# Linear attention into a multiplicative FFN: all loads on one queue, the weight fold first, full-height attention matmuls

## The chip, the cores and the metric

The kernel runs on one core of one Trainium2 chip. The metric is device time in microseconds: 260.99 us is the median of three executions of the kernel before (260.66 to 261.18). A profile of one execution has a span of 258.1 us, counted from its first to its last instruction; the measured time is 2.9 us longer than that span.

## The reference

Inputs are f32: q, k, v of shape (8 batches, 8 heads, 576 tokens, 64), w1 and w2 of shape (512, 1024), w3 of shape (1024, 1024), w_out of shape (1024, 512). The output is (4608, 512) in f32.

```python
def phi(x):
    return np.where(x > 0, x, np.exp(x) - 1.0) + 1.0
q_p, k_p = phi(q), phi(k)
kv  = np.einsum('bhsd,bhse->bhde', k_p, v)
z   = np.sum(k_p, axis=2)
num = np.einsum('bhsd,bhde->bhse', q_p, kv)
den = np.einsum('bhsd,bhd->bhs', q_p, z)[..., None] + 1e-06
attn = num / den                              # (8, 8, 576, 64)
x = attn.transpose(0, 2, 1, 3).reshape(4608, 512)
a, b = x @ w1, x @ w2
out = ((a * b) @ w3) @ w_out
```

Two things are used by both kernels. The last two products have nothing between them, so w3 @ w_out is multiplied once into a 1024x512 matrix `wf` (the fold), for which w3 must be transposed. And phi(x) = max(x + 1, min(exp(x), 1)) = min(max(x, 0) + 1, exp(x)).

## The kernel before

Each batch has 576 tokens: 512 are held as four tiles of 128 ("J", j = 0 to 3), the other 64 are the rest ("R"), and two rests make one more tile of 128. The 36 tiles go through the FFN in 9 chunks of 4. A list of steps, `ORDER`, fixes the order of the instructions on every engine; each engine executes its own in that order. The parts that the change touches:

```python
ld = ctx.enter_context(tc.tile_pool(name="ld", bufs=5))    # raw q, k, v of a batch, 1 MB each; w3 too
mm_ps = ... bufs=4   # PSUM, one bank each
at_ps = ... bufs=2   # PSUM, two banks each

def load_qkv(name, src, b, part, alt=False):     # q, k, v on SyncE's queue
    ...
    return nc.sync.dma_start(out=..., in_=src[b, h0:h1, 0:NJ * P, :]...)
def load_w12(x): ...  nc.gpsimd.dma_start(...)   # weights: GpSimd's queue, f32 to bf16 on the way
def load_wo(x):  ...  nc.gpsimd.dma_start(...)
def load_w3(i):  ...  nc.gpsimd.dma_start(...)

# phi: exp on ScalarE, then two steps on VectorE
nc.scalar.activation(out=e, in_=x, func=AF.Exp)                      # L137, 1024 elements, e in bf16
nc.vector.tensor_scalar_min(out=e, in0=e, scalar1=1.0)               # L141, bf16
nc.vector.scalar_tensor_tensor(                                      # L162, 256 elements, x in f32
    out=out, in0=x, scalar=1.0, in1=e, op0=ALU.add, op1=ALU.max)

def kv_half(b, g):     # batches 1 to 7: 64-row matmuls in pairs, two partial sums
    for n, (kk, vv, halves) in enumerate(steps):
        for r in halves:
            rows = slice(r * R, (r + 1) * R)
            nc.tensor.matmul(kvp[:, r, i * W:(i + 1) * W], kk[rows], vv[rows], ...)     # L199
    nc.scalar.copy(out=kvf, in_=kvp[:, 0, 0:2 * W])                                     # L203
    nc.vector.tensor_tensor(out=kvs[b]..., in0=kvf, in1=kvp[:, 1, 0:2 * W], op=ALU.add) # L204

def nat_units(b, js):  # numerator and denominator of a tile: 8 matmuls of 64 rows x 65 columns
    for hp in range(KC):
        for u in range(2):
            nc.tensor.matmul(nd[0:n, u, ...], w[rows], kvs[b][rows, hp, u, :], ...)     # L265
    # VectorE: add 1e-6 (L271), reciprocal (L273), multiply (L275), grouped for two tiles

def xt_tr(b, j): ...   # x transposed on TensorE (L285): batches 1 and 3
def xt_load(b, part): ... nc.sync.dma_start(out=dst, in_=src, transpose=True)   # batches 2, 4 to 7, rests
def q_tr(b, g): ...    # q transposed on TensorE (L309): batches 0 to 3; by DMA (qt_load) in 4 to 7
def first_nd(hp, own): # batch 0 alone: masked kv against q, the result is x already transposed
    ...                # L330; 1/den as exp(-ln(den)) on ScalarE

def f_unit(c, f):      # 4 matmuls for a, 4 for b (L371); a copied (L376); a * b on VectorE (L377)
def o_unit(c, m):      # 8 matmuls with wf (L390), copy to SBUF (L393), store on SyncE (L400)
def o_last(c, m):      # the last tile in two halves, stored on two queues (L417, L420)
def w3_tr(i): ...      # 8 transposes of w3 on TensorE (L454), copy (L455)
def wf_mm(i, part): .. # 8 matmuls, w3t against w_out (L464), copy (L467)
```

At the start, ORDER interleaves the load and the work of batch 0 with the fold: w3 rows 0 to 3 and w_out are asked for at the beginning, w3 rows 4 to 7, w1 and w2 later, beside q, k and v.

Of the kernel before, what the change touches and what calls it, by code (L numbers as in the profile page):

```python
# [13 lines left out]
P = 128  # L14
# [4 lines left out]
def kernel(  # L19
# [14 lines left out]
    NTOK = B * S  # L34
# [5 lines left out]
    JW = H * NJ * D  # L40
    RW = (H // 2) * D
    n_chunks = NTOK // NCH

# [3 lines left out]
    for b in range(0, B, 2):  # L47
        for key in [("J", b, j) for j in range(NJ)] + [("J", b + 1, j) for j in range(NJ)] + [("R", b, 0)]:
            tile_of[key] = len(order)
            order.append(key)  # L50
        tile_of["R", b + 1, 0] = tile_of["R", b, 0]
# [5 lines left out]
    ldr = ctx.enter_context(tc.tile_pool(name="ldr", bufs=8))  # L57
    setup = ctx.enter_context(tc.tile_pool(name="setup", bufs=2))
    phi_p = ctx.enter_context(tc.tile_pool(name="phi", bufs=1))
    e_p = ctx.enter_context(tc.tile_pool(name="e", bufs=2))  # L60
    att = ctx.enter_context(tc.tile_pool(name="att", bufs=2))
    lr = ctx.enter_context(tc.tile_pool(name="lr", bufs=2))
    ab_p = ctx.enter_context(tc.tile_pool(name="ab", bufs=2))
    sm = ctx.enter_context(tc.tile_pool(name="sm", bufs=3))
# [3 lines left out]

    ident = consts.tile([P, P], BF16)
    mask = consts.tile([P, 2, 2, D], BF16)  # L70
    eps = consts.tile([P, 1], F32)
    zero = consts.tile([P, NCH], BF16)

    w1_sb = wpool.tile([P, KC, DFF], BF16)
    w2_sb = wpool.tile([P, KC, DFF], BF16)
    wo_sb = wpool.tile([P, FC, DM], BF16)
    wf_sb = wpool.tile([P, FC, DM], BF16)
    xt = wpool.tile([P, NT, KC, P], BF16)
    vt = wpool.tile([P, NJ, H, D + 1], BF16)
    vr = wpool.tile([P, H // 2, D + 1], BF16)  # L80

    def constants(part):
        if part == 0:
            make_identity(nc, ident)
        elif part == 1:

            nc.gpsimd.memset(mask, 0.0)
            nc.gpsimd.memset(mask[0:D, :, 0, :], 1.0)
            nc.gpsimd.memset(mask[D:P, :, 1, :], 1.0)
            nc.gpsimd.memset(eps, 1e-6)  # L90
            nc.gpsimd.memset(vt[:, :, :, D:D + 1], 1.0)
            nc.gpsimd.memset(vr[:, :, D:D + 1], 1.0)
        else:
            nc.vector.memset(zero, 0.0)

    def warm_up(n):

        ps = mm_ps.tile([P, NCH], F32, tag="mm", name="warm")
        for _ in range(n):
            nc.tensor.matmul(ps, zero[:, 0:P], zero, start=True, stop=True)  # L100


    raw = {}

    def load_qkv(name, src, b, part, alt=False):


        if part == 3:
            t = raw[name + "r", b] = ldr.tile([P, RW], F32, tag="ldr", name=f"{name}32r")
            for hh in range(2):  # L110
                (nc.gpsimd if alt else nc.sync).dma_start(  # L111
                    out=t[hh * R:(hh + 1) * R].rearrange("p (h d) -> p h d", d=D),
                    in_=src[b, hh * 4:(hh + 1) * 4, NJ * P:S, :].rearrange("h p d -> p h d"))
            return None
        if (name, b) not in raw:
            raw[name, b] = ld.tile([P, JW], F32, tag="ld", name=f"{name}32")
        t = raw[name, b]
        h0, h1 = ((0, 4), (4, 8), (0, 8))[part]
        W = NJ * D
        return nc.sync.dma_start(  # L120
            out=t[:, h0 * W:h1 * W].rearrange("p (h x) -> p h x", x=W),
            in_=src[b, h0:h1, 0:NJ * P, :].rearrange("h (p j) d -> p h (j d)", j=NJ))


    ph = {}

    es = {}

    def phi_exp(name, b, g):

        if g == 2:
            x, e = raw[name + "r", b], e_p.tile([P, RW], BF16, tag="er", name="er")
        else:
            x = raw[name, b][:, g * (JW // 2):(g + 1) * (JW // 2)]
            e = e_p.tile([P, JW // 2], BF16, tag="e", name="e", bufs=4)
        es[name, b, g] = x, e
        nc.scalar.activation(out=e, in_=x, func=AF.Exp)  # L137

    def phi_min(name, b, g):
        e = es[name, b, g][1]  # L140
        nc.vector.tensor_scalar_min(out=e, in0=e, scalar1=1.0)  # L141

    def phi_max(name, b, hp):

        if (name, b) not in ph:
            ph[name, b] = [None, None]
        if hp == KC:
            dr = ph[name, b][1] = phi_p.tile([P, RW], BF16, tag=name + "r", name=name + "r", bufs=3)
            todo = [(dr, *es[name, b, 2])]
        else:  # L150
            if hp == 0:
                ph[name, b][0] = phi_p.tile([P, KC, NJ, 2, D], BF16, tag=name + "j", name=name + "j")
            dj = ph[name, b][0]
            x, e = es[name, b, hp // 2]
            W = NJ * D
            todo = []
            for u in range(2):
                h = 2 * (hp % 2) + u
                todo.append((dj[:, hp, :, u, :], *(t[:, h * W:(h + 1) * W].rearrange(
                    "p (j d) -> p j d", d=D) for t in (x, e))))  # L160
        for out, x, e in todo:
            nc.vector.scalar_tensor_tensor(  # L162
                out=out, in0=x, scalar=1.0, in1=e, op0=ALU.add, op1=ALU.max)

    def copy_of(alt):
        return nc.vector.tensor_copy if alt else nc.scalar.copy

    def v_unit(b, i, alt=False):

        if i < 2:  # L170
            copy_of(alt)(  # L171
                out=vt[:, :, 4 * i:4 * i + 4, 0:D],
                in_=raw["v", b].rearrange("p (h j d) -> p j h d", h=H, j=NJ)[
                    :, :, 4 * i:4 * i + 4])
        else:
            copy_of(alt)(out=vr[:, :, 0:D], in_=raw["vr", b].rearrange("p (h d) -> p h d", d=D))


    kvs, qts, xns = {}, {}, {}

    def kv_half(b, g):


        kj, kr = ph["k", b]
        if g == 0:
            kvs[b] = att.tile([P, KC, 2, D + 1], BF16, tag="kv", name="kv")
        kvp = at_ps.tile([P, 2, 512], F32, tag="at", name="kvp")
        W = 2 * (D + 1)
        for i in range(2):
            hp = 2 * g + i  # L190
            steps = [(kj[:, hp, j].rearrange("p u d -> p (u d)"),
                      vt[:, j, 2 * hp:2 * hp + 2, :].rearrange("p h e -> p (h e)"), (0, 1))
                     for j in range(NJ)]
            steps.append((kr[:, i * P:(i + 1) * P],
                          vr[:, 2 * i:2 * i + 2, :].rearrange("p h e -> p (h e)"), (g,)))
            for n, (kk, vv, halves) in enumerate(steps):
                for r in halves:
                    rows = slice(r * R, (r + 1) * R)
                    nc.tensor.matmul(  # L199
                        kvp[:, r, i * W:(i + 1) * W], kk[rows], vv[rows],  # L200
                        start=(n == 0), stop=(n == (NJ if r == g else NJ - 1)))
        kvf = lr.tile([P, 2 * W], F32, tag="kvf", name="kvf")
        nc.scalar.copy(out=kvf, in_=kvp[:, 0, 0:2 * W])  # L203
        nc.vector.tensor_tensor(  # L204
            out=kvs[b][:, 2 * g:2 * g + 2].rearrange("p a u e -> p (a u e)"), in0=kvf,
            in1=kvp[:, 1, 0:2 * W], op=ALU.add)

    def kv_full(b, g):

        kj, kr = ph["k", b]  # L210
        if g == 0:
            kvs[b] = att.tile([P, KC, 2, D + 1], BF16, tag="kv", name="kv")
        kvp = at_ps.tile([P, 2, 512], F32, tag="at", name="kvp")
        W = 2 * (D + 1)
        rows = slice(g * R, (g + 1) * R)
        for i in range(2):
            hp = 2 * g + i
            for j in range(NJ):
                nc.tensor.matmul(kvp[:, 0, i * W:(i + 1) * W],
                                 kj[:, hp, j].rearrange("p u d -> p (u d)"),  # L220
                                 vt[:, j, 2 * hp:2 * hp + 2, :].rearrange("p h e -> p (h e)"),
                                 start=(j == 0), stop=False)
            nc.tensor.matmul(kvp[:, 0, i * W:(i + 1) * W], kr[rows, i * P:(i + 1) * P],
                             vr[rows, 2 * i:2 * i + 2, :].rearrange("p h e -> p (h e)"),
                             start=False, stop=True)
        return kvp[:, 0, 0:2 * W]

    def kv_copy(b, g, p, alt=False):
        copy_of(alt)(out=kvs[b][:, 2 * g:2 * g + 2].rearrange("p a u e -> p (a u e)"), in_=p)


    def qt_load(b, part):
        qj, qr = ph["q", b]
        if part == 0:
            t = att.tile([P, KC, NJ * P], BF16, tag="qt", name="qt")
            src = qj.rearrange("p c j u d -> p (c j u d)")
            dst = t.rearrange("p c (j t) -> p (c j) t", t=P)
        else:
            t = att.tile([P, 2, P], BF16, tag="qtr", name="qtr", bufs=3)
            src, dst = qr, t  # L240
        qts[b, part] = t
        nc.sync.dma_start(out=dst, in_=src, transpose=True)

    def nat_units(b, js):


# [384 lines left out]
```

## Time and profile before

| | busy us | share of the span |
|---|---|---|
| TensorE matmul (PE) | 237.4 | 92% |
| TensorE weight load (PEld) | 116.2 | 45% |
| VectorE (DVE) | 167.9 | 65% |
| ScalarE (ACT) | 129.0 | 50% |
| GpSimd (POOL) | 21.1 | 8% |

HBM read is 38.80 MB, written 9.44 MB. The queue table counts 48.98 MB, as the bytes land: weights are read as f32 and land as bf16, at half their size, and transposes by DMA inside the chip are counted too. The page cuts the span into 40 slices of 6.45 us, with a digit for the busy tenths of each engine in each; matmuls are pipelined, so the spacing of their starts says more than the length of one. TensorE's granted clock is full in all slices.

### The profile page before, as it was taken

What the parts mean: (1) busy time and instruction counts of PE and PEld (TensorE: products, weight loads), DVE (VectorE), ACT (ScalarE), POOL (GpSimd) and SP (SyncE); (2) the same over time, 40 slices, a digit from 0 to 9 for tenths busy, and PEclk for the clock granted to TensorE, in tenths of its full rate; (3) what the DMA queues carried; (4) which work ended last, traced back from release to release, by engine and by line L of the source; (5) the groups of instructions that cost most, each with busy time, mean ns of one, the idle gap of its engine ahead of it and who ended that gap; (6) DMA issues with size and microseconds to landing.
All of it is one profiled execution on the core that took longest, in us unless ns stands there. A gap on an engine that the chain in (4) does not pass through costs nothing.

```text
span 258.1 us, 4507 instructions
## 1 busy us (share of the span) xinstructions
PE 237.4 (92%) x1656; PEld 116.2 (45%) x1673; DVE 167.9 (65%) x426; ACT 129.0 (50%) x205; POOL 21.1 (8%) x42
## 2 busy tenths in 40 slices
PE   1138999999999999999999999999999999999994
PEld 1124554545454454455444444444444444444442
DVE  0025787969978979997968589468866543423320
ACT  2048587858478664677353645726533203331421
POOL 8000765000101000000000000000000000000000
PEclk9999999999999999999999999999999999999999
DMA  6999999999898599939988975934980124003024
GB/s 100 200 257 378 316 229 245 208 334 307 302 291 250 87 340 215 307 104 253 211 193 245 369 160 123 248 99 131 218 220 26 34 57 124 0 37 125 3 82 163
DMA packets 70085, 48.98 MB, mean 190 GB/s; under 512 B 34416, under 2 KB 64368, under 8 KB 70064
## 3 DMA queue, kind: packets, MB, share of 16 engines
q1 hardware_dynamic: 63104, 42.54, 61.4%
q0 software_dynamic: 6816, 6.03, 14.1%
q8 instruction: 13, 0.21, 0.3%
q10 hardware_dynamic: 144, 0.13, 0.1%
q14 instruction: 8, 0.07, 0.1%
HBM read 38.80 MB, written 9.44 MB: 187 GB/s over the span
## 4 chain that ended last, share of the span: by engine, by line
PE 84%; DMA 8%; ACT 2%; SPq 1%; issue 1%; DVE 1%; DVEq 0%; POOLq 0%
PE a_ps L371 25%; PE b_ps L371 24%; PE o_ps L390 23%; DMA k<-in_k_dram 4%; DMA w3b<-in_moe_w_dram 4%; PE kvp L199 3%; PE wf_ps L464 3%; PE nd L265 3%; SPq L111 1%; PE tp L309 1%; PE w3p L454 1%; PE xtp L285 1%; PE o_ps L417 1%; DVE qj L162 1%; ACT e L137 0%
## 5 line engine op out<-in xcount | busy, mean ns | idle before, releaser
L371 PEld LDWEIGHTS <-w_sb 128*128 128x128 bf16 x576 | 54.2, 98 | 63.4 <-issue 0.5
L377 DVE TENSOR_TENSOR ab<-a_sb,b_ps 128x512 bf16<-128x512 f32 x72 | 49.0, 684 | 46.6 <-PE b_ps L371 35.4
L371 PE MATMUL a_ps<-xt,w_sb 128*128 128x512 bf16 x288 | 75.1, 380 | 0.1
L371 PE MATMUL b_ps<-xt,w_sb 128*128 128x512 bf16 x288 | 74.9, 379 | 0.0
L376 ACT COPY a_sb<-a_ps 128x512 f32<-128x512 f32 x72 | 41.9, 586 | 56.8 <-PE a_ps L371 55.6
L390 PE MATMUL o_ps<-wf_sb,ab 128*128 128x512 bf16 x266 | 63.2, 379 | 0.7
L390 PEld LDWEIGHTS <-ab 128*128 128x128 bf16 x280 | 26.7, 98 | 30.8
L393 ACT COPY o_sb<-o_ps 128x512 f32<-128x512 f32 x24 | 14.0, 583 | 30.7 <-PE o_ps L390 30.7
L162 DVE SCALAR_TENSOR_TENSOR kj<-k,e 128x256 bf16<-128x256 f32 x64 | 23.6, 417 | 0.1
L162 DVE SCALAR_TENSOR_TENSOR qj<-q,e 128x256 bf16<-128x256 f32 x64 | 23.4, 417 | 0.1
L141 DVE TENSOR_SCALAR e<-e 128x1024 bf16<-128x1024 bf16 x32 | 13.4, 420 | 14.2 <-ACT e L137 14.2
L137 ACT ACTIVATE e<-q 128x1024 bf16<-128x1024 f32 x16 | 16.7, 1058 | 9.3 <-DMA q<-in_q_dram 9.1
L454 PE MATMUL w3p<-ident,w3b 128*128 128x128 bf16 x64 | 6.1, 253 | 15.0 <-ACT w3t L455 8.0
L137 ACT ACTIVATE e<-k 128x1024 bf16<-128x1024 f32 x16 | 16.9, 1056 | 4.1 <-DMA k<-in_k_dram 2.7
L275 DVE TENSOR_TENSOR xn<-nd,r 128x512 bf16<-128x512 f32 x28 | 18.0, 686 | 0.0
L464 PE MATMUL wf_ps<-wo_sb,w3t 128*128 128x512 bf16 x61 | 16.7, 412 | 1.0 <-ACT w3t L455 0.8
L454 PEld LDWEIGHTS <-w3b 128*128 128x128 bf16 x64 | 4.9, 113 | 16.6 <-DMA w3b<-in_moe_w_dram 8.2
L393 DVE COPY o_sb<-o_ps 128x512 f32<-128x512 f32 x11 | 7.6, 688 | 6.4 <-PE o_ps L390 6.4
L171 ACT CAST vt<-v 128x1024 bf16<-128x1024 f32 x9 | 9.3, 1046 | 2.0 <-DMA v<-in_v_dram 2.0
L203 ACT COPY kvf<-kvp 128x260 f32<-128x260 f32 x14 | 5.3, 375 | 8.9 <-PE kvp L199 8.7
L464 PEld LDWEIGHTS <-w3t 128*128 128x128 bf16 x64 | 6.2, 104 | 7.8 <-issue 1.7
L199 PE MATMUL kvp<-vt,kj 64*128 64x130 bf16 x224 | 9.2, 217 | 0.0
(81 smaller groups left out, 163.5 us busy)
## 6 DMA issues: line engine op xcount, KB each, us to landing
out_dram<-o_sb SPq DMA_DIRECT2D x31, 256.0 KB, 3.2
k<-in_k_dram SPq DMA_DIRECT2D x7, 1024.0 KB, 8.6
q<-in_q_dram SPq DMA_DIRECT2D x7, 1024.0 KB, 8.2
v<-in_v_dram SPq DMA_DIRECT2D x6, 1024.0 KB, 7.4
w3b<-in_moe_w_dram POOLq DMA_DIRECT2D x8, 256.0 KB, 7.1
v<-in_v_dram SPq DMA_DIRECT2D x4, 512.0 KB, 8.5
w_sb<-in_moe_w_dram POOLq DMA_DIRECT2D x8, 256.0 KB, 11.3
out_dram<-o_sb SPq DMA_DIRECT2D x9, 128.0 KB, 2.4
```

The costliest lines, as they stand in the source:

```text
L137: nc.scalar.activation(out=e, in_=x, func=AF.Exp)
L141: nc.vector.tensor_scalar_min(out=e, in0=e, scalar1=1.0)
L162: nc.vector.scalar_tensor_tensor(out=out, in0=x, scalar=1.0, in1=e, op0=ALU.add, op1=ALU.max)
L199: nc.tensor.matmul(kvp[:, r, i * W:(i + 1) * W], kk[rows], vv[rows], start=(n == 0), stop=(n == (NJ if r == g else NJ - 1)))
L275: nc.vector.tensor_tensor(out=dst.rearrange("p (c u) e -> p u c e", u=2), in0=v4[:, :, :, 0:D], in1=r[0:n].unsqueeze(3).to_broadcast([n, 2 ...
L371: nc.tensor.matmul(ps, w[:, kc, f * P:(f + 1) * P], xt[:, 4 * c:4 * c + 4, kc, :], start=(kc == 0), stop=(kc == KC - 1))
L376: nc.scalar.copy(out=a_sb, in_=a_ps)
L377: nc.vector.tensor_mul(out=abs_[c][:, f, :], in0=a_sb, in1=b_ps)
L390: nc.tensor.matmul(o_ps, ab[:, f, m * P:(m + 1) * P], wf_sb[:, f, :], start=(f == 0), stop=(f == FC - 1))
L393: copy_of(alt)(out=o_sb, in_=o_ps)
L454: nc.tensor.transpose(tp[:, kc, :], raw["w3", i][:, kc * P:(kc + 1) * P], ident)
L464: nc.tensor.matmul(wfs[i], w3ts[i][:, kc, :], wo_sb[:, kc, :], start=(kc == 0), stop=(kc == FC - 1))
```

## The change

The kernel is written anew around the same arithmetic, with a new ORDER. Its parts:

1. All loads, of q, k, v as well as of weights, are issued from GpSimd's queue, in one order. SyncE's queue keeps transposes and stores.
2. The fold is first: w3 rows 0 to 3, then w_out in four slices; after each slice, four rows of `wf` are taken a step further (`wa`). The other four rows follow when their w3 has landed. Short matmuls on zeros (`warm`) fill the first waits.
3. Attention matmuls use all 128 rows: kv in one accumulation per pair of heads with the rest padded by zeros (`vrz`), and numerator and denominator of a pair of heads together against a block-diagonal `kvb` (130 columns).
4. TensorE transposes q and x for batches 0 to 3, also x of batches 0 and 2; DMA transposes serve batches 4 to 7 and the rests. Batch 0 is computed as the others are.
5. phi is computed as min(max(x, 0) + 1, exp(x)): one step from f32 to bf16, one on two bf16 tensors.

The purpose is to have TensorE start the fold as soon as its data lands, to keep waiting stores and transposes out of the way of loads, and to save a copy and an addition per kv.

```diff
-def load_qkv(...):   nc.sync.dma_start(...)            # 1 MB, 512 KB and 64 KB pieces
+def ld_(n, b, h0, nh, queue):   queue_of[queue].dma_start(...)    # always "g", nc.gpsimd
+def lr(n, b, queue):            # the rest of a batch in one piece of 128 KB
-nc.vector.tensor_scalar_min(out=e, in0=e, scalar1=1.0)
-nc.vector.scalar_tensor_tensor(out=out, in0=x, scalar=1.0, in1=e, op0=ALU.add, op1=ALU.max)
+nc.vector.tensor_scalar(out=d, in0=raw, scalar1=0.0, scalar2=1.0, op0=ALU.max, op1=ALU.add)   # t, 1024
+nc.vector.tensor_tensor(out=d[:, hp], in0=ts, in1=es, op=ALU.min)                             # m, 512, bf16
-kv_half: 36 matmuls of 64 rows a batch, ACT copy and DVE add for each half
+def kv(b, hp):  5 matmuls of 128 rows x 130 columns (4 tiles and the padded rest), 4 of these a batch
+def kc(b, g0, ng, r, eng):  two copies a batch into the diagonal blocks of kvb
-nat_units: 8 matmuls of 64 rows x 65 columns a tile; VectorE's steps grouped for two tiles
+def na(b, hp):  4 matmuls of 128 rows x 130 columns, 4 of these a batch (nar: 4 for the rest)
+def nd(b, hp):  add 1e-6, reciprocal, multiply, one unit at a time
-first_kvz, first_nd, first_rest (batch 0)
+def xp(b, hp), xc(b, hp, eng):  x transposed on TensorE for batches 0 to 3
+def wa(c0, n):  rows 0 to 3 of wf against slices c0 .. c0 + n of w_out
-L0.3 E0 I0 M0.0 x0.2 N0.3 E1 X0.0 w0 y0.2 M1.3 E2 w1 L0.0 ...
+l3:0 const:0 const:6 l3:1 warm:26,0 ... l3:3 lo:0,2 lo:2,2 w3t:0 warm:8,1 lo:4,2 w3c:0,a lo:6,2 ...
+ld:k,0,0,4,g ... lr:k,0,g ... lr:v,0,g wa:0,1 ld:k,0,4,4,g wa:1,1 ... ld:q,0 (2) ... ld:v,0 (3) ...
+l3:6 ... l3:7 ... lw:0,0 lw:1,0 lw:0,1 lw:1,1 ... lw:1,3 ... ld:k,1 lr:k,1 ... lr:v,1 ... ld:q,1 ... ld:v,1 (2)
+... kv:0 ... na:0 nd:0 xp:0 xc:0 ... fk:0,0 f:0,3 f:0,5 f:0,4 f:0,6 f:0,2 f:0,7 f:0,1 qt:1,0 kv:1,0 ...
-... Q8.2
+... ol:8,2 oc:7,1,a st:7,1,s o:8,1 oc:8,1,v st:8,1,s      # the last tile in one piece
```

(`l3` loads a row block of w3, `lo` a slice of w_out, `lw` a quarter of w1 or w2, `ld` and `lr` q, k, v; `f` is a unit of w1 and w2, `o` of wf, `oc` its copy, `st` its store. Most of ORDER and all definitions not spoken of are left out.)

## The prediction

> **What bounds the kernel now.** I read the page's 40 slices first, then the chain of waits in order of time, then the cadence of TensorE in the timeline.
>
> ```profile
> PE   1138999999999999999999999999999999999994
> DVE  0025787969978979997968589468866543423320
> DMA  6999999999898599939988975934980124003024
> GB/s 100 200 257 378 316 229 245 208 334 307 302 291 250 87 340 215 307 104 253 211 193 245 369 160 123 248 99 131 218 220 26 34 57 124 0 37 125 3 82 163
> ```
>
> PE is at 9 from the fifth slice to the last but one. The only slices in which it is not are the first four, up to 25.8 us, in which the DMA engines are full. The chain says the same in time (start, length, what):
>
> ```profile
> 1.24 3.78 DMA w3b<-in_moe_w_dram
> ...
> 9.04 11.36 DMA k<-in_k_dram
> ...
> 25.29 6.50 DMA w3b<-in_moe_w_dram
> ...
> 245.99 6.64 PE o_ps L390 x30
> 252.63 1.76 PE o_ps L417 x16
> ```
>
> So a load ends last until 31.8 us, and after that nearly only TensorE. Is a busy PE at its own rate? The timeline (start, length, what) answers:
>
> ```profile
> 118.27 1.03 PE L371 MATMUL b_ps<-xt,w_sb 128*128 128x512 bf16 x4
> 119.23 0.40 PE L199 MATMUL kvp<-vt,kj 64*128 64x130 bf16 x8
> ...
> 120.35 1.90 PE L390 MATMUL o_ps<-wf_sb,ab 128*128 128x512 bf16 x7
> 122.19 0.42 PE L265 MATMUL nd<-kv,qt 64*128 64x65 bf16 x16
> 122.54 1.04 PE L371 MATMUL a_ps<-xt,w_sb 128*128 128x512 bf16 x4
> 123.41 1.03 PE L371 MATMUL b_ps<-xt,w_sb 128*128 128x512 bf16 x4
> 124.28 1.03 PE L371 MATMUL a_ps<-xt,w_sb 128*128 128x512 bf16 x4
> ```
>
> From 122.54 to 124.28 there are 8 matmuls of 512 columns: 0.216 us each, 0.42 ns a column. Between full-height groups, a batch's kv takes 119.13 (the start 118.27 plus 4 x 0.216) to 120.35, 1.22 us; two tiles of nd take 0.46 us (one of the 8 o_ps records before them is missing from the trace).
>
> All work of PE, in these units: 576 matmuls of w1 and w2, 124.3; 288 of wf, 62.2; 64 of the fold, 13.8; 160 transposes at 0.056 (four take 108.90 to 109.13), 8.9; batch 0 by its own way, 3.1; kv and nd of seven batches, 7 x (1.22 + 2 x 0.46 + 0.34 for the rest) = 17.4; sum 229.7. The last matmul ends at 254.4, so 24.7 us are idle or slow, nearly all before 32 us. That is all the change can win at PE, unless it reduces PE's work.
>
> **What the Trainium skill says.** (1) "TensorEngine Tiling (Array Packing)", section Key Properties: changing the tiling mode drains TensorE. The trace agrees: 0.10 us lie between 119.13 and 119.23, and as much before 122.19. (2) "VectorE: DVE Perf Modes", section What auto-detection actually checks: an operation with a single source in SBUF takes two elements a cycle even in f32, one with two 16-bit sources two as well. For the first the trace agrees: 1024 elements of v, f32 to bf16, take VectorE 0.70 us (and bf16 to bf16 0.42), where 512 from PSUM take 0.69. The second is in no row of before. (3) "DMA: Bandwidth & Descriptors", section Issuing engines are not separate DMA queues: the queues share the same 16 engines, so another queue brings no bandwidth. No stretch of before has GpSimd's queue alone, so the rate of that queue by itself is my largest unknown.
>
> **The change part by part.**
>
> PE's work. kv is 20 matmuls of 130 columns a batch, at 0.0567 us each 1.13; na is 16 of these, 0.91; nar 4, 0.23; sum 2.27 instead of 2.48. Eight batches make 18.2. Transposes become 192 (w3, q and x 64 each), 10.7. With 186.5 for w1, w2, wf and 13.8 for the fold: 229.2. So full height saves 1.5 us in seven batches, batch 0 0.8, and the added transposes give 1.8 back. PE's sum doesn't move; only idle time can.
>
> VectorE. Two minima of 0.42 and 8 steps of 0.42 for each of k and q, 8.4 us a batch, become four steps of 0.70 and eight of 0.42 (taking the skill's rate), 6.2 us. kv loses two additions, nd isn't grouped any more and costs some 0.15 us more per unit, xc has twice as many copies. Summed by steps of ORDER, from chunk 1 to the beginning of chunk 2 VectorE has 29.7 us of instructions beside 26.0 us of PE; as instructions overlap by 0.08 us (four of 0.417 take 1.42), it is 26. So VectorE isn't the bound, but has no slack from 64 to 90 us, and about 2 us in each later batch up to 135.
>
> The start, where the gain is. At what rate does data arrive? Eight slices of 6.45 us sum to 12.5 MB landed by 51.6 us; in them all weights landed as 5.2 MB in bf16, for which 10.5 MB were read. So 17.7 MB were read from about 3 us on: 364 GB/s. HBM to SBUF alone has this too (GB/s in the last column):
>
> ```profile
> 6.00:9.00 3.00, 1.14 (x9) 0.77 (x8) 0.02 (x1) 0.00 (x0) 0.62 (x4) 1.00 1.08 158
> 18.00:21.00 3.00, 3.00 (x8) 1.03 (x7) 0.00 (x0) 0.57 (x1) 0.00 (x0) 1.00 1.09 383
> ```
>
> The new order of loads in MB read, added up: w3 0 to 3, w_out, w3 4 and 5: 5.2; k0 and two rests: 6.6; q0: 7.6; v0: 8.65; w3 6, 7: 9.7; four quarters of w1 and w2: 10.7, 11.8, 12.8, 13.9; k1, rests, q1, v1: 17.3. At 364 GB/s from 3 us v0 lands at 26.8, the second quarter at 35.4, the fourth at 41.2, v1 at 50.5; I add up to 1.5 us for the small rests (the first window above, where such pieces move, has only 158).
>
> Chunk 0 begins after v0 at about 27.5: cast 1.1, kv 1.1, copies 0.5, four nd of 1.03, xc and transposes some 2: about 36.5, where the second quarter is there too. In before it begins in part at 43.7 and in full at 49.6. It takes 8 x 1.73 = 13.8, and a transpose of q 0.9: 51.2. Then kv of batch 1 waits for v1 at 52 and its cast, 1.05: **53**. So PE is bound by v1's landing by about 2 us, not by the fold, which lies in the wait for q, k and v.
>
> From there PE has: 512 matmuls of w1 and w2, 110.5; 288 of wf, 62.2; attention of batches 1 to 7, 15.9; nar 0.2; 40 transposes of q and 48 of x, 4.9. Sum 193.7, PE ends at 246.7. The end is a bit longer: a whole tile is copied (0.69 instead of 0.37 us) and stored in one piece (3.2 from issue to landing, instead of 1.9); I take 4.5 instead of 3.7. Span 251.2, time 254.1 with the 2.9 between span and time. After 49.6 us before itself loses 1.0 us of PE beyond its sums (203.8 of work, 204.8 of time); for a VectorE without slack I put 1.5: **255.5 us**, 5.5 less than before.
>
> Off the path: loads no longer wait behind stores on SyncE's queue (25.1 us in total in the waits of that queue), but no wait of PE in before comes from q, k or v after 32 us, so I give this nothing.
>
> **Rivals.**
>
> (a) GpSimd's queue alone is slower. The first loads are read at about 245 GB/s in 3 to 9 us, and the change has no second queue to fill gaps. At 300 GB/s v1 lands at 60.7, PE ends 8 us later than above: 263. Against it: casts were in flight in most of the 51.6 us that gave 364. One in six.
>
> (b) VectorE becomes the bound from 60 to 135 us. For: the sums above, 26 beside 26. If a third of the 40 nd units leave PE waiting for 0.3 us, and each batch adds 0.5, it is 4 to 8 us, and 259 to 262. Against: in before VectorE is at 19.18 of 20 us from 100 to 120, and PE waits for nothing. One in four for a good part of it.
>
> (c) The start is better than I think: data at 385 GB/s, as in 18 to 21 us. Then v1 lands at 48, and chunk 0's own chain, 51.2, binds: 252. One in four.
>
> (d) The loads are hidden anyway: before has also 17.7 MB to read, and at 52 us has 202.4 us still to go (254.4 less 52), after has about 194 at 53. The difference of some 7 us is therefore the whole gain, whatever PE does earlier, and stalls eat into it.
>
> **Range and chances.** 2% lies at 255.8, just above my number. Rival (c) sets the lower end with some luck in stalls, (a) or (b) the upper: 249.5 to 262. Below 255.8 in 52 of 100; within 2% (to 266.2) in 42, most of it from (b); slower in 6, for (a) and (b) together.
>
> **What would show it.** The windows to 30 us give the rate of the one queue: 360 or 300. The first a_ps should start near 36.5 us, the first kvp of batch 1 near 53, and the chain should name v there. From then on PE's cadence should be 0.216 with idle time under 3 us in all; idle time of PE released by DVE would be (b). kv of a batch should be 1.13 us with no gap of 0.1 before it. m should take 0.42 us; were it 0.69, VectorE would gain 2.2 us a batch and bind, and the number would be wrong by 10 us. Loads that arrive late after 60 us would show as waits for DMA on ACT or DVE.

## The result, and the profile after

The changed kernel takes 285.83 us (median of four executions, 285.39 to 291.59), the kernel before 260.84 us on the same chip. The ratio is 1.094, with an interval of 1.090 to 1.097: **9.4% slower**, where 255.5 us was predicted and 262 was the upper end.

The 40 slices of the changed kernel, each now 7.1 us wide, rows as in the prediction and the granted clock of TensorE besides:

```profile
PE   6793899891699999989917997899999999999993
DVE  4009645982499975499915955997735511333101
PEclk9999599998699999999996999999999999999999
DMA  6999999999999999847999886339500331010133
GB/s 105 190 237 335 198 244 273 240 288 263 383 309 222 288 292 275 79 125 206 195 145 302 139 235 117 76 72 237 63 0 18 76 111 47 28 71 6 74 131 129
```

Before, TensorE was at 9 from the fifth slice on. Now the first slices are fuller (6, 7 and 9 instead of 1, 1 and 3), in part with the short matmuls on zeros, and the first product of w1 (`a_ps`) starts at 40.41 instead of 43.69. But there are holes: "1" in the tenth slice (64 to 71 us) and "1" in the twenty-first (142 to 149 us), each with a clock of 6 in the slice behind it, and a soft stretch (7 and 8) from 171 to 185 us. The fifth slice has a clock of 5. In both holes the DMA engines stand at 9.

The chain of waits names what ended last (start, length, what):

```profile
51.66 13.59 DMA q32r<-in_q_dram
...
67.03 14.80 DMA v32r<-in_v_dram
...
132.08 18.56 DMA qt<-q
150.69 1.05 PE nd L285 x8
151.74 1.71 PE a_ps L389 x4
...
164.80 9.02 DMA qt<-q
```

For the first hole the chain runs over two loads of rests, for the second over `qt<-q`, the transpose of a batch's phi(q) by DMA. That took 4.9 us in the median before and never more than 6.5; here one took 18.6. For the rests of q (`qtr<-qr`) it is 13.4 us in the median instead of 4.8. The waits of TensorE (total, times, longest) say what that cost:

```profile
PE ndr L310 <- DMA qtr<-qr: 8.6, 1, 8.6
PE nd L285 <- DMA qt<-q: 7.8, 1, 7.8
PE qtp L261 <- DVE q L174: 4.8, 2, 3.4
```

And the timeline of TensorE shows the second of them (start, length, line, operation; in brackets the idle time ahead and who ended it):

```profile
141.86 1.03 PE L389 MATMUL b_ps<-xt,w_sb 128*128 128x512 bf16 x4
150.69 1.05 PE L285 MATMUL nd<-kvb,qt 128*128 128x130 bf16 x8 [7.80 <-DMA qt<-q]
151.53 1.91 PE L389 MATMUL a_ps<-xt,w_sb 128*128 128x512 bf16 x4
153.24 1.87 PE L389 MATMUL b_ps<-xt,w_sb 128*128 128x512 bf16 x4
154.94 0.40 PE L285 MATMUL nd<-kvb,qt 128*128 128x130 bf16 x4
```

Besides the 7.8 us of waiting, the four matmuls of a_ps behind it start 1.71 us ahead of those of b_ps, where 0.86 is usual: TensorE runs at half clock for 4.3 us after the wait.

Idle time of TensorE by stretches (20 us less its busy time in the windows) puts the loss in place:

| us | 60–80 | 80–100 | 100–120 | 120–140 | 140–160 | 160–180 | sum |
|---|---|---|---|---|---|---|---|
| before | 0.05 | 0.11 | 0.05 | 0.16 | 0.05 | 0.05 | 0.5 |
| after | 8.65 | 0.88 | 0.48 | 1.42 | 7.86 | 2.13 | 21.4 |

**The theory (A).** In before, the loads of q, k and v and the DMA transposes shared SyncE's queue. The change put the loads on GpSimd's queue. The DMA engines serve the two queues in turn, one packet each; a packet of a transpose carries 256 B, one of an f32 load on GpSimd's queue 4096 B. The transpose then crawls. The DMA view of the changed kernel for 70 to 72 us (packets, MB, share of 16 engines), inside the first hole:

```profile
q0 software_dynamic: 160, 0.63, 96.0%
q1 hardware_dynamic: 158, 0.04, 12.6%
```

q0 is GpSimd's queue with the loads, q1 SyncE's with the transpose: 160 packets against 158, and 0.63 MB against 0.04. The page "DMA: Bandwidth & Descriptors" of the Trainium skill states this in its section Queues, rings and completion order: an engine goes round between the queue rows it has work for, packet by packet. The trace agrees.

**Rivals:** (B) the loads themselves come late, because one queue carries them all (the chain through the first hole speaks for it); (C) VectorE, which had no slack on paper, holds TensorE up.

### The profile page after: what moved, and what is told of

Its sections match the earlier page's. It is cut to its first block, busy times and chain, and to the rows that moved or that the text cites. A ratio compares the mean times of both kernels' runs of the same rounds, so it can differ in the third digit from the quotient of the medians.

```text
span 284.3 us, 4032 instructions
## 1 busy us (share of the span) xinstructions
PE 244.4 (86%) x1490; PEld 128.1 (45%) x1506; DVE 161.8 (57%) x360; ACT 129.6 (46%) x192; POOL 57.5 (20%) x79
## 4 chain that ended last, share of the span: by engine, by line
PE 49%; DMA 27%; DVE 14%; issue 4%; POOL 2%; ACT 1%; DVEq 0%; SPq 0%; POOLq 0%
PE a_ps L389 15%; PE b_ps L389 15%; PE o_ps L414 12%; DMA qt<-q 10%; DMA v32r<-in_v_dram 5%; DMA q32r<-in_q_dram 5%; DMA q<-in_q_dram 4%; DMA wo<-in_moe_w_out_dram 3%; DVE t L166 3%; DVE ab L408 2%; PE kvp L232 2%; DVE xn L293 2%; DVE k L174 2%; DVE q L174 1%; PE nd L285 1%
## 5 line engine op out<-in xcount | busy, mean ns | idle before, releaser
L414 PE MATMUL o_ps<-wf_sb,ab 128*128 128x512 bf16 x267 | 64.3, 382 | 1.1 <-DVE ab L408 0.4
L285 PE MATMUL nd<-kvb,qt 128*128 128x130 bf16 x128 | 12.7, 235 | 10.5 <-DMA qt<-q 7.8
L166 DVE TENSOR_SCALAR t<-k 128x1024 bf16<-128x1024 f32 x16 | 10.9, 686 | 15.6 <-DMA k<-in_k_dram 15.6
L174 DVE TENSOR_TENSOR q<-t,e 128x512 bf16<-128x512 bf16 x32 | 12.4, 420 | 11.4 <-DMA qt<-q 11.1
L122 POOL DMA_DIRECT2D k<-in_k_dram x9 | 7.8, 862 | 53.5 <-ACT vt L211 21.6
L285 PEld LDWEIGHTS <-qt 128*128 128x128 bf16 x128 | 9.4, 104 | 16.0 <-DMA qt<-q 8.3
L211 ACT CAST vt<-v 128x1024 bf16<-128x1024 f32 (+1 forms) x13 | 13.2, 1015 | 1.6 <-PE kvp L232 1.3
L232 PE MATMUL kvp<-vt,k 128*128 128x130 bf16 x128 | 12.0, 231 | 2.2 <-DVE k L174 1.1
L122 POOL DMA_DIRECT2D v<-in_v_dram x11 | 9.6, 869 | 14.0 <-ACT vt L211 3.5
L174 DVE TENSOR_TENSOR k<-t,e 128x512 bf16<-128x512 bf16 x32 | 12.2, 417 | 0.2
L232 PEld LDWEIGHTS <-k 128*128 128x128 bf16 x128 | 9.5, 103 | 5.5 <-DVE k L174 1.7
## 6 DMA issues: line engine op xcount, KB each, us to landing
k<-in_k_dram POOLq DMA_DIRECT2D x7, 1024.0 KB, 10.5
q<-in_q_dram POOLq DMA_DIRECT2D x7, 1024.0 KB, 13.5
v<-in_v_dram POOLq DMA_DIRECT2D x3, 512.0 KB, 13.8
```

Source lines behind the costliest of these rows:

```text
L122: return queue_of[queue].dma_start(out=t[:, h0 * W:(h0 + nh) * W].rearrange("p (h x) -> p h x", x=W), in_=src[n][b, h0:h0 + nh, 0:NJ * P, ...
L166: nc.vector.tensor_scalar(out=d[:, 0:nh * W], in0=raw[n, b][:, h0 * W:(h0 + nh) * W], scalar1=0.0, scalar2=1.0, op0=ALU.max, op1=ALU.add)
L174: nc.vector.tensor_tensor(out=d[:, hp].rearrange("p j u d -> p u j d"), in0=ts[n, b, h0][:, s].rearrange("p (u j d) -> p u j d", u=2, j=NJ ...
L232: nc.tensor.matmul(dst, kj[:, hp, j].rearrange("p u d -> p (u d)"), vt[:, j, 2 * hp:2 * hp + 2, :].rearrange("p h e -> p (h e)"), start=(j ...
L285: nc.tensor.matmul(o[:, j // 2, (j % 2) * 256:(j % 2) * 256 + PW], sb["qt", b][:, hp, j * P:(j + 1) * P], kvb[b % 3][:, hp].rearrange("p u ...
L414: nc.tensor.matmul(d, sb["ab", c][:, f, m * P:(m + 1) * P], wf_sb[:, f, :], start=(f == 0), stop=(f == FC - 1))
```

## The experiments

All times are medians; a ratio is to the kernel before on the same chip, with its 95% interval. In `ORDER`, the last letter of a load `ld` (q, k or v of a batch) or `lr` (its rest) is the queue: g is GpSimd's, s SyncE's. `qt`/`xp` transpose by TensorE, `qd`, `xd`, `qdr`, `xdr` by DMA.

### The disputed cost by itself (e6)

This kernel computes nothing of the reference (its output is zeros). It transposes one tile of 512 KB by DMA on SyncE's queue five times: alone; beside six f32 loads of 1 MB on GpSimd's queue; beside the same loads cast to bf16; beside the f32 loads on ScalarE's queue; and behind two loads in SyncE's own queue.

```diff
+ phases = ((None, 0, False), (nc.gpsimd, 6, False), (nc.gpsimd, 6, True),
+           (nc.scalar, 6, False), (nc.sync, 2, False))      # queue, loads, cast
+ for n, (queue, count, cast) in enumerate(phases):
+     for i in range(count): load(queue, i, cast)
+     nc.sync.dma_start(out=dst_t[n]..., in_=src_t[n], transpose=True)
```

> Not the computation: only one DMA transpose of 512 KB from SyncE's queue, five times one after the other, (1) alone, (2) with six loads of 1 MB as f32 from GpSimd's queue begun some 4 us before it, (3) the same loads cast to bf16, (4) the same loads as f32 from ScalarE's queue, (5) two such loads ahead of it in SyncE's own queue; the output is filled with zeros. Theory A: from issue to landing (1) 4 to 5 us, (2) 15 us or more, up to the end of the loads, (3) 7 to 12, (4) 8 to 12, as 1 KB packets are in the way, (5) 4 to 10, what the loads before it need. If only bandwidth were shared, whatever the packets, (2), (3) and (4) would be alike and under 10 us. If a transpose weren't slowed by loads at all, all five would be 4 to 5.

From issue to landing: alone 4.3 us; beside the f32 loads on GpSimd's queue **19.5**; beside cast loads 15.2; beside the loads on ScalarE's queue 12.6; behind two loads in its own queue 4.8. The DMA view for 37 to 41 us (f32 loads on GpSimd's queue) and then for 83 to 87 us (ScalarE's queue, q10):

```profile
q0 software_dynamic: 345, 1.31, 93.3%
q1 hardware_dynamic: 345, 0.09, 10.9%
```

```profile
q10 hardware_dynamic: 1138, 1.15, 80.9%
q1 hardware_dynamic: 1140, 0.29, 32.1%
```

The counts of packets are equal each time; what differs is how many there are in 4 us, 345 with packets of 4096 B against them and 1140 with packets of 1 KB. The transpose needs 2048 packets of 256 B; beside the f32 loads it got about half of them through one for one, and the other 1016 from 43 to 45 us, when the loads were done. So the 19.5 us are in large part the length of the loads. Cast loads came out worse than the 7 to 12 us expected: their 512 B packets go at 963 in 4 us, no faster than the 1 KB packets of ScalarE's queue. Besides, beside loads the transpose's first packet moves only 4 to 5 us after its issue, alone after 1 to 2; that part is not explained by taking turns. The mechanism of A is shown; it is not the whole delay, and its size depends on the packets on the other side.

### Loads on SyncE's queue again, or in smaller packets (e1, e9 and e2)

All loads of q, k and v from the weights on go back to SyncE's queue:

```diff
- lr:q,0,g ... ld:v,1,0,4,g ... ld:q,2,0,8,g ...      # every load behind lw:1,3
+ lr:q,0,s ... ld:v,1,0,4,s ... ld:q,2,0,8,s ...
```

> Loads of q, k, v of batches 1 to 7 on SyncE's queue, at the same places of ORDER; weights and batch 0 stay on GpSimd's. Theory A (the transposes by DMA on SyncE's queue get one small packet of 256 B for each packet of 4 KB of GpSimd's queue, so they take 9 to 19 us while loads are under way): with loads in 1 KB packets in the transposes' own ring, a transpose lands in 4 to 7 us, PE's waits for qtr and qt fall from 16.4 us to under 4, and the time is 255 to 265. Rival B (one in-order queue of loads with waits for buffers brings q, k, v too late): SyncE's queue is just as much in order and has stores in it besides, so loads come later still and the time is 285 or more. Rival C (VectorE has no slack from 60 to 135 us): nothing of VectorE changes, the time stays within 3 us of 285.8.

272.58 us, ratio 1.043 (1.038 to 1.048). No wait for a transpose is left (the median of qtr is 5.9 us instead of 13.4), but 255 to 265 was missed. The kv of batch 1 starts at 63.9 us instead of 56.5: the first transposes of q are 2.5 us later, and TensorE waits 3.7 us for weights. So I put only the loads that batches 2 to 7 need on SyncE's queue:

```diff
- ld:v,1,0,4,g ld:v,1,4,4,g lr:q,0,g lr:q,1,g ld:v,2,0,8,g ld:k,2,0,8,g ...
+ ld:v,1,0,4,g ld:v,1,4,4,g lr:q,0,s lr:q,1,s ld:v,2,0,8,s ld:k,2,0,8,s ...
```

> After with the loads of q, k and v from the rests of q on (what batches 2 to 7 read) on SyncE's queue, the queue of the transposes, as before has it; batch 0 and 1 stay on GpSimd's queue. Theory A: the start is that of after (first a_ps at about 40.5), transposes land in 4 to 7 us from 58 us on, no wait of TensorE for qt or qtr above 2 us: 260 to 267, better than e1's 272.6, whose start was late. Rival B (loads behind stores and transposes come late, which was the reason for the change): waits of ACT and DVE for loads reach TensorE, 270 or more.

272.96 us, ratio 1.044 (1.039 to 1.049): missed again, and with the same number. The DMA view for 40 to 44 us tells why:

```profile
q1 hardware_dynamic: 681, 0.68, 61.9%
q0 software_dynamic: 683, 0.34, 61.5%
```

It is the same rule, against another victim. q1 now carries loads of batch 2, which nothing needs yet; q0 carries casts of w1 and w2, with q and v of batch 1 behind them, which are needed now, in packets half the size. Each takes its turn, so the urgent ones get a third of the bytes; the quarters take 13.5 us to land in the median (9.3 in after), and kv of batch 1 starts at 62.4, its second half at 64.3. One queue for all loads has a use of its own: it keeps the order of need.

Next, the loads stay on GpSimd's queue but cast to bf16 on the way, which makes their packets 512 B:

```diff
- t = got(raw, (n, b), ld, [P, H * W], F32, "ld", f"{n}32")
+ t = raw[n, b] = ... ld.tile([P, H * W], F32, ...).bitcast(BF16)[:, 0:H * W]      # rests likewise
```

> All loads stay on GpSimd's queue in the same order, but q, k, v are cast to bf16 on the way, as the weights are; the trace shows such packets to be of 512 B at most, instead of 4 KB. Theory A: [...]the transposes land in 5 to 10 us instead of 7 to 19, PE's waits for qtr and qt fall to under 7 us, the time is 262 to 274 (small packets may slow the loads themselves at the start by 2 to 4 us). Rival B: nothing of queue and order changes, the waits stay, 283 or more. Rival C: VectorE's step t from bf16 takes 0.42 instead of 0.69 us, 1.1 us less a batch, so the time falls by 4 to 8 us, with PE's waits for DVE going down and those for qt and qtr staying.

267.73 us, ratio 1.023 (1.018 to 1.028), as A expected. TensorE's waits for transposes fall to 5.1 us. VectorE and ScalarE get bf16 to read here, so this alone doesn't separate A from C.

### Taking the transposes off the DMA engines (e3 and e4)

First those of the rests only (qdr, xdr), which TensorE does instead, with ScalarE's copy; then all of them, 160 transposes more by TensorE:

```diff
-        nc.sync.dma_start(out=d, in_=ph["qr", p, 2], transpose=True)
+        for c in range(KC):
+            nc.tensor.transpose(t[:, c, :], ph["qr", p, 2][:, c * P:(c + 1) * P], ident)
+        nc.scalar.copy(out=d, in_=t)
```

> The transposes of the rests (qdr, xdr) are done by TensorE and copied by ScalarE; those of whole batches 4 to 7 stay with DMA. Theory A: the wait of 8.6 us at 65 us disappears with the slow clock after it (1.2 us), the wait at 143 us stays; TensorE has 32 transposes more, 1.8 us; the time is 275 to 279. Rival B: the loads behind that wait are unchanged, TensorE waits for them shortly after, and less than 4 us are won: 282 to 286. Rival C: as B, and ScalarE's added copies change nothing.

> After without any transpose by DMA: those of q and x of batches 4 to 7 and of all rests are done by TensorE too, with their copies on ScalarE and VectorE. It adds 160 transposes by TensorE, 160 x 0.056 = 9.0 us of its work, and 24 copies. Theory A: all waits for qt, qtr, xt by DMA are gone; 285.8 - 29 + 9 = 266 to 272, with 3 to 6 us of that from VectorE. Rival B (loads themselves are late): 280 or more, as the loads are unchanged.

The first takes 278.18 us, ratio 1.068 (1.061 to 1.076), in the range: the hole at 65 us is gone, the one for `qt` is there with 4.0 us. The second takes 279.27, ratio 1.069 (1.064 to 1.073), where A said 266 to 272 with the added work counted in, and B 280: closer to B. No wait for a transpose by DMA is left, and TensorE is busy for 254.5 us instead of 244.4. If all 9.0 us of added work lengthen the time, it stands at 270 without them; by this estimate 15 us of the 25 lost to before are the transposes', some 10 are not.

### Only the times of four loads (e7 and e8)

Here nothing is moved to another queue or engine. Four loads are held until a given transpose has landed; as GpSimd's queue is executed in order, the loads behind a held one start later too (none is issued from 57.2 to 66.8 us, where after issues two, at 58.44 and 61.50):

```diff
- ld:q,2,0,8,g mr:q,0,2 kc:1,0,2,1,a m:q,1,4,3 qdr:0
+ mr:q,0,2 kc:1,0,2,1,a m:q,1,4,3 qdr:0 ld:q,2,0,8,g
- GATES = ""
+ GATES = "ld:q,2,0,8,g<qdr:0 ld:q,6,0,8,g<qd:4 ld:q,7,0,8,g<qdr:3 ld:k,7,0,8,g<qd:5"
```

> The changed kernel with four loads started later: the f32 loads of q for batches 2, 6 and 7 and of k for batch 7 wait until one named transpose (of the q rests of batches 0 and 1, of q of batch 4, of the q rests of batches 6 and 7, of q of batch 5) has landed. Queue, size and type of every transfer stay as they are in after; only these four times change. Theory A (a 256 B packet of a transpose on SyncE's queue is served one for one with a 4096 B packet of a load on GpSimd's queue): the four transposes land in 4 to 9 us, the waits of TensorE for qtr and qt (8.6 and 7.8 us in after) fall below 2 us each, the time is 262 to 270. Rival B (the loads are late as it is, their sum is what binds): later loads make it worse, 285 or more.

271.02 us, ratio 1.039 (1.034 to 1.043): 1 us above the expected range, and 15 us faster than after, by starting loads **later**. Rival B falls with it. The transpose of q of batch 4 lands in 4.3 us instead of 18.6, that of the first q rests in 7.6 instead of 14.8, and TensorE's waits for DMA are

```profile
PE ndr L310 <- DMA qtr<-qr: 1.4, 1, 1.4
```

and nothing more for a transpose. With e4 (less its added work) two quite different edits leave the same 270 to 271 us. TensorE's idle time from 60 to 180 us is still 8.8 us, and VectorE ended nearly all of what is not this wait.

Gates and casts together:

```diff
+ both edits: bf16 loads of q, k, v, and the GATES above
```

> The edits of e2_cast_loads (q, k, v cast to bf16 by the load, so in packets of 512 B or less) and of e7_gated together. Theory A: what the cast leaves of the waits for qt and qtr (5.1 us) goes for the most part; 258 to 264, below e2's 267.7, and about level with before. Rival C (what is left of e2's loss is VectorE without slack, not the transposes): 265 to 269, no better than e2.

259.19 us, ratio 0.991 (0.989 to 0.994): under the kernel before, and 12 us under e7. What do those 12 us consist of, data or VectorE?

### VectorE: relieved, and loaded (e11 and e12)

In the gated f32 kernel e7, the copies of o and x and the casts of v that VectorE has from 57 us on (chunks 0 to 4) are moved to ScalarE:

```diff
- oc:0,0,v ... v:2,0,4,v ... xc:1,0,v oc:0,3,v ...
+ oc:0,0,a ... v:2,0,4,a ... xc:1,0,a oc:0,3,a ...
```

> e7_gated with work moved from VectorE to ScalarE from 57 us on: the copies of o of chunks 0 to 4 that VectorE has (11), its copies of x (6) and its two casts of v go to ScalarE, some 11 us of VectorE's instructions; nothing else is changed. If what is left between e7 (271.0) and e8 (259.2) is VectorE without slack (rival C, 0.70 us for a step on f32 where a step on bf16 takes 0.46), this is 3 to 6 us faster than e7: 265 to 268. If it is the loads themselves (twice the bytes in SBUF, late data), VectorE's relief gives nothing: 270 to 272, or more where ScalarE's copies come late.

271.08 us, ratio 1.039 (1.035 to 1.044): no gain. It seemed to clear VectorE, but the timeline of VectorE in e7 shows that the test missed its mark. From 67.6 to 91 us, where VectorE has no gap, it executes steps t and m, the products ab and xn; there isn't one of the moved copies among them. Later the copies did leave VectorE, and TensorE's idle time from 60 to 180 us was 10.1 us, not less than e7's 8.8. So e11 speaks neither for C nor clears VectorE. The reverse: the fastest kernel (e10, below) with one more VectorE instruction of 0.29 us behind each t, into a tile that nothing reads, which gives VectorE the load of f32 inputs while the transfers stay as they are:

```diff
         scalar1=0.0, scalar2=1.0, op0=ALU.max, op1=ALU.add)
+        nc.vector.tensor_scalar(out=extra, in0=d[:, 0:512], scalar1=0.0, scalar2=1.0, op0=ALU.max, op1=ALU.add)
```

> e10_cast_gated_half with one more VectorE instruction behind each step t of q and k: the same operation on 512 elements a partition into a tile that nothing reads, 0.29 us, 32 times, 9.3 us in all. With it VectorE has the load that f32 inputs give it (0.69 us for t instead of 0.42), while the transfers stay those of e10. If a VectorE without slack is what separates e7 from e8, the time goes from 257.5 to 261 or more, with waits of TensorE for ab, q and k in 64 to 100 us. If it is the transfers alone, it stays below 259.5.

263.96 us, ratio 1.009 (1.005 to 1.012), 6.5 us above the same kernel without it (5.5 by the ratios, each to the kernel before on its own chip). Windows of this one and then of the kernel without the additions (stretch, its length, busy time of PE, PEld, DVE, ACT and POOL, granted clock, DMA share, GB/s):

```profile
80.00:100.00 20.00, 19.04 (x139) 10.52 (x138) 15.43 (x41) 15.12 (x21) 7.68 (x10) 1.00 1.53 201
100.00:120.00 20.00, 18.89 (x126) 9.84 (x124) 14.16 (x35) 11.46 (x19) 0.89 (x1) 1.00 0.77 102
```

```profile
80.00:100.00 20.00, 19.89 (x137) 10.77 (x137) 12.86 (x33) 13.84 (x21) 7.16 (x10) 1.00 1.52 212
100.00:120.00 20.00, 19.34 (x139) 10.84 (x140) 16.39 (x43) 15.40 (x25) 1.06 (x1) 1.00 0.80 125
```

TensorE loses 0.9 and 0.5 us there, and 3.3 us in all from 60 to 180 (5.9 us idle instead of 2.6); the first a_ps is 1.9 us later, as batches 0 and 1 have the added steps too and TensorE's longer wait for q (3.36 us instead of 2.18) is followed by half clock. So VectorE's load is worth somewhat less than half of the 13.5 us between e7 and the kernel without the additions, with no transfer changed. C is a second cause, not a rival. What makes up the other half isn't tested.

### The queue alone, in the kernel before, and the lead in the changed one (e13 and e5)

The kernel before with this part of the change and no other:

```diff
-        return nc.sync.dma_start(
+        return (nc.gpsimd if b >= 2 else nc.sync).dma_start(      # rests likewise
```

> The kernel before with one part of the change alone: the loads of q, k and v of batches 2 to 7 are issued on GpSimd's queue instead of SyncE's. The instructions of TensorE, VectorE and ScalarE and their order are those of before; size, type and number of all transfers too. Theory A (a small packet of a transpose is served one for one with a 4096 B packet of a load once they are in two queues): the median of a transpose of q goes from 4.9 us in before to 8 us or more, single ones to 15, waits of TensorE for qt and qtr appear, the time is 268 to 290. Rival (what slows the transposes in after is the new order or the new place of the steps, not the queue): transposes at 5 us, 260 to 262.

260.78 us, ratio 0.998 (0.996 to 1.000). **A as I had put it falls here**: in most executions the queue alone costs the kernel before nothing. Three of the 20 took 266.5 to 275.6 us, though, where none of 26 of the kernel before took more than 263.0; no trace of the three was kept, so whether transposes stalled in them is open. The transposes do slow down, from 4.9 to 7.6 us in the median (8 or more was expected), as the DMA issues of both kernels from 102 to 116 us show, before first, then this one (count, us from issue to landing):

```profile
qt<-qj SPq DMA_TRANSPOSE x1, 6.0
```

```profile
qt<-qj SPq DMA_TRANSPOSE x1, 9.5
```

But nobody waits for it in this trace. The first matmul on it comes at 123.92, and its issue was at 106.41: 17.5 us of lead, as in before (104.68 and 122.19). In the changed kernel the lead is 6.0 us for the first q rests (issue 58.88, TensorE ready at 64.9) and 10.6 for q of batch 4 (132.08 and 142.7, the end of the last matmul ahead of the wait). Besides, loads of a batch land sooner here, 8.2 to 8.7 us after issue in the median where those of the changed kernel take 10.5 to 14.0, and no transpose of q takes more than 9.5. So the lead and the loads beside it both differ, and e13 doesn't separate them. I moved the first uses in the changed kernel:

```diff
- xp:1,0 o:0,3 xc:1,1,a st:0,2,s nd:1,3 xc:1,0,v nar:1 oc:0,3,v xp:1,3 xp:1,2 nar:0 ...
+ xp:1,0 o:0,3 xc:1,1,a st:0,2,s nd:1,3 xc:1,0,v oc:0,3,v xp:1,3 xp:1,2 ...
+ ... m:k,3,0,1 nar:1 nar:0 ndr:1 ndr:0 xdr:0 f:1,3 ...
```

> The changed kernel with five steps moved: the attention of the rests of batches 1 and 0 (nar:1, nar:0), their division and their transpose back (ndr, xdr:0) come some 15 us of TensorE's work later, so that the first use of the transposed q rests lies some 20 us behind its issue instead of 6. Loads, queues and transposes are those of after. If it is the short lead in the new order that turns a slow transpose into a stall: the transpose still takes 12 to 16 us, the wait of 8.6 us for it is gone or below 1 us, the slow clock after it too, and the time is 274 to 278; the waits at 142 and from 164 us on stay as they are. If TensorE loses the time anyway (late loads or a full VectorE behind the transpose): above 281.

285.72 us in the median, without an interval and in a wide range: one of the four executions took 275.3, in the expected range, the other three 284.9 to 287.3, as expected if TensorE loses the time anyway. The trace is of one of these three, with a clock of 0.948 on the mean. The transpose of the first q rests takes 15.0 us, as in after, and nobody waits for it. SyncE issues the transpose of q of batch 4 at 126.78 instead of 132.08, 5.3 us ahead of after, and there TensorE loses them again:

```profile
150.76 1.05 PE L285 MATMUL nd<-kvb,qt 128*128 128x130 bf16 x8 [13.18 <-DMA qt<-q]
```

That transpose takes 23.9 us now instead of 18.6. A longer lead removes this one wait, as expected; the gain can be taken back by the next transpose that meets loads. Why the execution of 275.3 us escaped that isn't shown, as its trace wasn't kept.

### A version that beats both (e10)

Gates and casts, with the load of q of batch 7 held until q of batch 5 is transposed (in e8 that transpose took 9.3 us), and the last tile in two halves:

```diff
- ld:q,7,0,8,g<qdr:3        ol:8,2 ... o:8,1 oc:8,1,v st:8,1,s
+ ld:q,7,0,8,g<qd:5         o:8,2 ... oc:8,2,v st:8,2,s ol:8,1
```

> A version meant to beat both kernels. e8_cast_gated with the load of q of batch 7 held until the transpose of q of batch 5 has landed (in e8 that transpose takes 9.3 us beside it and TensorE waits 2.35 us and then runs 2.5 us at half clock), and with the last tile computed, copied and stored in two halves, as before has it. Theory A: 2.35 + 2 us of e8's loss go, the end is 0.6 us shorter: 254 to 257.5. If the transpose of q of batch 5 is still slow for another reason (v of batch 7 or stores in flight), 258 to 260, as e8.

257.48 us, ratio 0.988 (0.985 to 0.990), at the upper end of what was expected: 1.2% faster than the kernel before and 10% faster than the changed one. Its slices:

```profile
PE   6996699979999999999999998999999999999994
PEclk9999999999999999999999999999999999999998
DMA  6999999997999999396997994792014221020144
```

No hole is left, and no slice with a slow clock. The transpose of q of batch 5 takes 4.5 us, and the idle time of TensorE from 60 to 180 us is 2.6.

## Why the prediction was wrong, point by point

**Sizes of the steps: right.** kv of a batch takes 1.13 us (84.58 to 85.71) with no gap ahead; m takes 0.42 us and t 0.69, as assumed; chunk 0's products take 13.8 us (40.41 to 54.2); the cadence of TensorE is 0.216 us a matmul wherever it isn't held up; the end from the last matmul on takes 4.6 us (279.7 to 284.3), where 4.5 was predicted. So TensorE's sum of 229 us isn't in question.

**The start: 3.5 us too early.** kv of batch 1 starts at 56.53, not 53. The failed term is the 9 us from chunk 0's beginning (27.9, predicted 27.5) to the first a_ps: it took 12.5. One candidate is the clock:

```profile
27.00:30.00 3.00, 2.04 (x24) 1.78 (x25) 2.88 (x8) 2.67 (x4) 2.30 (x4) 0.77 1.10 252
30.00:36.00 6.00, 4.99 (x48) 4.26 (x47) 3.31 (x12) 1.77 (x5) 3.58 (x6) 0.54 1.42 195
```

TensorE had waited 3.38 us for q up to 27.9 and was granted half clock (0.77 and 0.54 in the column behind POOL) up to 35.4. I had sized kv and nd at full clock. But e10 shows the same stretch at a clock of 1.00 throughout (inputs in bf16):

```profile
25.05 0.62 PE L261 MATMUL qtp<-ident,q 128*128 128x128 bf16 x8 [2.18 <-DVE q L174]
36.75 0.59 PE L389 MATMUL a_ps<-xt,w_sb 128*128 128x512 bf16 x2
```

That is 11.7 us, so half clock accounts for about 0.8 of the 3.5. What I had left out is the rest of the fold: "which lies in the wait for q, k and v" fails for its last two row blocks, whose 16 transposes and 16 matmuls (4.4 us at full rate) stand in this stretch, from 32.72 on in after, the last of them ending where a_ps starts. No run takes them out, so their share of the 3.5 us isn't measured. "PE is bound by v1's landing" failed too: ahead of kv of batch 1 TensorE waits 1.38 us for VectorE's q, not for v.

**"For a VectorE without slack I put 1.5": this is the term that failed.** From kv of batch 1 to the last matmul 193.7 us of work took 223.2; the stalls are 29.5 us, not 1.5. Their sum, from the trace: 8.6 + 7.8 = 16.4 waiting for transposes; some 1.3 + 2.1 = 3.4 lost to half clock behind these two waits (2.7 and 4.3 us of work at 0.50); 6.3 in eleven waits for VectorE; the remaining 3.4 in pieces too small to name.

Two sentences carried the error. "The queues share the same 16 engines, so another queue brings no bandwidth" is true of sums, and nothing here contradicts it; but I read from it that a queue doesn't matter, while the same page says how the engines are shared, by turns of packets. And "loads no longer wait behind stores on SyncE's queue ... I give this nothing" looked at the loads alone. I counted what the change takes off that queue and never asked what stays there: the transposes, in 256 B packets, now against 4096 B ones. The page of before counts 34416 of its 70085 packets under 512 B: the small packets were there to be seen. That f32 loads go in 4096 B packets on GpSimd's queue was in no view of before that I read.

The third omission is the lead. Transposes of up to 9.5 us cost nothing in the old order, which leaves them 17.5 us (e13); the new order uses them 6 to 11 us after issue, beside more loads. How much of the stalls is due to the lead and how much to the loads isn't separated: e5 lengthened one lead, and only one of its four executions gained; e7 took loads away and gained 15 us. I took the new order to be free, because its work is the same.

**Rivals.** (a), a slower queue, didn't bind: starting loads later made the kernel faster. (b), VectorE as the bound, I put at 4 to 8 us and one in four: e12 gives 5.5 to 6.5 us for the load that f32 inputs put on it, so its size was right, and my 1.5 should have been this. (c), a faster start, failed with the 12.5 us above, whatever the rate of the loads. (d) is right as far as it goes: whatever the start gave, stalls ate.

## What to carry to other kernels

Moving loads to another queue doesn't only free the old one: ask what remains in it, how large its packets are against those of the new neighbour, and how long after issue its result is needed. What is urgent and small can share a queue with its rivals (4.8 us behind two loads in e6), or its rivals can be held until it has landed; holding loads back gained 15 us here. And a step whose engine has "no slack" on paper should be priced by loading that engine on purpose, not by a guess of 1.5 us.

## What the runs showed of the hardware

A transpose of 512 KB by DMA takes 4.3 us alone, 12.6 beside 1 KB packets on ScalarE's queue, 15.2 beside 512 B packets and 19.5 beside the f32 loads of GpSimd's queue; two busy queues had the same number of packets within 2% in each window shown, whether their packets carried 256, 512, 1024 or 4096 B. The same access pattern went in 1024 B packets on SyncE's and ScalarE's queues and in 4096 B packets on GpSimd's: the 7872 packets of q0 in e6 are what six loads of 1 MB make at 4096 B and six of 512 KB at 512 B, with 16 more for each of the twelve. The issue of such a transpose itself can hold its queue: 6.5 us for the one at 132.08, and 13.5 in the microbenchmark.

A wait of 8 us costs TensorE more than 8 us: the clock stood at 0.50 for 2.7 us of work after the wait at 65 and for 4.3 after the one at 143. The page "TensorE: Matmul & The Clock Gate" of the Trainium skill, section What's actually happening, says that an idle window of about 3.4 us puts the clock at half; both waits here were longer than twice that and were followed by it, while the waits of 1.4 us in e7 at 66 and of 1.1 in e10 at 51 were not. In between it goes either way: waits of 2.2 us ahead of the first transposes of q were followed by half clock in e2 and e8 and not in e10. And the clock column can miss it: in before, behind a wait of 8.0 us, eight matmuls of 512 columns take 3.42 us (17.70 to 21.12), 0.43 each, where the column says 1.00.
